# Rows of two batches in one output tile: interleaved on alternate partitions, or one batch in each half

## The chip, the cores and the metric

The kernel runs on one core of a Trainium2 chip. The metric is the device time of one execution in microseconds (us). Eight runs of the kernel before have a median of 428.32 us (427.91 to 428.47).

## What is computed

Sliding-window causal attention over 8 batches, 8 heads, 576 positions and 64 channels per head, followed by a spectral mixing layer. Cut to what matters:

```python
scores = q @ k^T / sqrt(64), kept where 0 <= i - j < 64
x = softmax(scores) @ v                    # as (batch 8, position 576, channel 512)
X = np.fft.rfft(x, axis=1)
Yr = Xr @ w_r[m] - Xi @ w_i[m]             # for the 64 lowest modes m, 512 x 512 each
Yi = Xr @ w_i[m] + Xi @ w_r[m]
y = np.fft.irfft(Y, n=576, axis=1)
u = x + y
out = u + np.maximum(u @ w_ch, 0.0)        # w_ch is 512 x 512
```

All inputs and the output are float32. The output is 8 x 576 x 512, 9.4 MB; the mode weights `w_r` and `w_i` are 64 matrices of 512 x 512 each.

## The kernel before

**Row tiles.** A batch has 576 positions: four whole tiles of 128 and a remainder of 64. The remainders of two neighbouring batches, `b` even and `b + 1`, share one tile, the *pair tile*, numbered `t = NT - 1 = 4` of the even batch. So there are 36 row tiles: 32 whole ones and four pair tiles.

**Stages.** First attention for all batches, then a Fourier transform into `XQ`. Next come the modes: for each mode two weight tiles of 512 KB (in bf16, cast on the way) are fetched by the GpSimd queue through a ring of buffers, and TensorE multiplies them (line 563, and 762 for the last four modes). Beside the modes run smaller jobs: `channel(i)` computes `x @ w_ch` for a row tile into `Z0`; `spectrum(b)` turns a batch's finished modes into the tiles `Yb` and `yw` that the inverse transform multiplies; `spread` rearranges `x_sb` (see below). When the last weights have been used, the *output stage* begins (from line 845), whose order on all engines is written out by hand.

**Output stage.** For row tile `n` of the list `seq`, `lay(n)` puts the tile's `Z0` into a PSUM bank, `rectify(n)` adds `trigI` times `yw` on TensorE (line 870) and takes the positive part on ScalarE (line 875), and `finish(n)` adds `trigI` times `Yb` on TensorE, adds `x_sb` on VectorE (line 893) into the SBUF tile `ot`, and issues the transfer of `ot` to the output on the sync queue (SP). `rectify` runs three tiles ahead of `finish`. In `seq` the pair tiles stand at n = 8, 13, 22 and 27. The pool of `ot` has seven tiles of 4 KB per partition.

**Whole tiles and their transfers.** Two whole row tiles are stored together: partition `p` holds positions `2p` and `2p + 1` of 256, so that each partition sends 4 KB in a row (line 900, 512 KB). The table `trigI` is laid out for that order, and `spread(b, h)` brings `x_sb` into it with four matmuls and two copies for each 256 positions, in the modes from `M0 = 48` to `ME = 60`.

**The pair tile before.** Partition `2s` holds position `512 + s` of the even batch and partition `2s + 1` the same position of the odd one. Four things make it so. `channel` reads the transposed tile with alternating halves (line 592 and 593). The columns of `trigI` from 512 on hold a zero at each even offset and position `512 + s` at offset `2s + 1` (lines 677 to 682); `add` takes 128 columns from 513 for the even batch and from 512 for the odd one (line 869), so that each batch's matmul adds zero to the other's partitions. `spread_pair(b)` rearranges `x_sb` with one matmul against a permutation, `turn`, and one copy (lines 779 to 787). And `finish` sends the tile with one transfer of 128 rows of 2 KB, whose destination alternates between the two batches (line 895).

**The sends.** `send(b)` moves eight rows of 4 KB from the tile `yl` to the last eight partitions of batch `b`'s `Yb` and `yw`, also on the sync queue (line 859). Batch 2 is sent before the first `finish`; `turn_of` (line 909) puts the others after n = 1, 5, 9, 12 and 15. TensorE needs them when it first rectifies a tile of that batch.

Of the kernel before, what the change touches and what calls it, by code (L numbers as in the profile page):

```python
# [9 lines left out]
FP32 = mybir.dt.float32  # L10
FP32R = mybir.dt.float32r
BF16 = mybir.dt.bfloat16
# [8 lines left out]
def view(ap, off, dims):  # L21

    return bass.AP(ap.tensor, ap.offset + off, [list(ap.ap[0])] + [list(d) for d in dims])
# [3 lines left out]
def kernel(  # L27
# [10 lines left out]
    nc = tc.nc  # L38
    B, H, S, D = q.shape
    NM = moe_w_r.shape[0]  # L40
    DM = moe_w_ch.shape[0]
# [3 lines left out]
    NT = 5  # L45
    NC = DM // 128
# [8 lines left out]
    def evac(o, i, on_act):  # L55

        if on_act:
            return nc.scalar.copy(out=o, in_=i)  # L58
        return nc.vector.tensor_copy(out=o, in_=i)  # L59
# [4 lines left out]
    wl = ExitStack()  # L64
# [3 lines left out]
    ident_bf = consts.tile([128, 128], BF16, name="ident_bf")  # L68
# [437 lines left out]
    M0 = L0 * MG  # L506
# [65 lines left out]
    with ExitStack() as p2a:  # L572
# [4 lines left out]
        def channel(i):  # L577
            b, t = tiles[i]
            n = 1 if t == NT - 1 else 2
            psts = []  # L580
            for k in range(n):
                pst = ps_t.tile([128, NC, 128], BF16, name="pxt")
                for c in range(NC):
                    nc.tensor.transpose(out=pst[:, c, :], in_=x_sb[:, b, t + k, 128 * c:128 * c + 128],  # L584
                                        identity=ident_bf)
                psts.append(pst)
            for j in range(n):
                xT = xtp.tile([128, NC, 128], FP32R, name="xT")
                for k in range(n):
                    w = 128 // n  # L590
                    nc.vector.tensor_copy(out=xT[:, :, w * k:w * k + w],  # L591
                                          in_=view(psts[k], j, [[128, NC], [n, w]] if n > 1 else
                                                   [[128, NC], [1, 64], [64, 2]]))
                psz = ps_z.tile([128, DM], FP32, name="psz")
                for c in range(NC):
                    nc.tensor.matmul(out=psz, lhsT=xT[:, c, :], rhs=wch[:, c, :],  # L596
                                     start=(c == 0), stop=(c == NC - 1))
                nc.scalar.copy(out=channel_out(i + j), in_=psz)  # L598
            return n
# [3 lines left out]
        for m in range(L0 * MG):  # L603
# [13 lines left out]
            if m == Z_M - 2:  # L617

                with tc.tile_pool(name="tmpi", bufs=1, reuse_waits="tile") as tmp:
# [23 lines left out]
                    for tab, row in ((trigI, pcol),):  # L643
                        fa, fb = floor(2 * MG, row, "fa"), floor(MG, row, "fb")

                        gcol, mcol = col("gcol"), col("mcol")
                        nc.vector.scalar_tensor_tensor(out=gcol, in0=fa, scalar=-2.0, in1=fb,
                                                       op0=ALU.mult, op1=ALU.add)
                        nc.vector.tensor_tensor(out=mcol, in0=fa, in1=fb, op=ALU.subtract)
                        nc.vector.scalar_tensor_tensor(out=mcol, in0=mcol, scalar=float(MG), in1=row,  # L650
                                                       op0=ALU.mult, op1=ALU.add)
                        for at, dg, dm in ((112 + ML, 1.0, -float(ML)), (112 + MG, -1.0, float(MG)),
                                           (112 + 2 * ML, -1.0, 0.0), (112 + 2 * ML + NLM, 1.0, -float(NLM))):
                            step = col("step")
                            nc.vector.tensor_single_scalar(out=step, in_=row, scalar=at - 0.5, op=ALU.is_ge)
                            nc.vector.scalar_tensor_tensor(out=gcol, in0=step, scalar=dg, in1=gcol,
                                                           op0=ALU.mult, op1=ALU.add)
                            if dm:
                                nc.vector.scalar_tensor_tensor(out=mcol, in0=step, scalar=dm, in1=mcol,
                                                               op0=ALU.mult, op1=ALU.add)  # L660
                        coef, coefs, coefc = col("coef"), col("coefs"), col("coefc")
                        nc.vector.tensor_single_scalar(out=coef, in_=mcol, scalar=0.0, op=ALU.is_equal)
                        nc.vector.tensor_scalar(out=coef, in0=coef, scalar1=-1.0 / S, scalar2=2.0 / S,
                                                op0=ALU.mult, op1=ALU.add)
                        nc.vector.tensor_tensor(out=coefs, in0=gcol, in1=coef, op=ALU.mult)
                        nc.vector.tensor_tensor(out=coefc, in0=coef, in1=coefs, op=ALU.subtract)
                        for i in range(NT):
                            n = SW if i < NT - 1 else 64
                            mt2 = tmp.tile([128, 2, SW], FP32, name="mti")[:, :, 0:n]
                            mt = mt2[:, 0, :]  # L670
                            nc.vector.tensor_scalar(out=mt, in0=pos[:, 0:SW] if n == SW else pos[:, SW:],
                                                    scalar1=float(256 * (i // 2) + i % 2) if n == SW else 0.0,
                                                    scalar2=mcol, op0=ALU.add, op1=ALU.mult)
                            tis = tmp.tile([128, SW], FP32, name="tis")[:, 0:n]
                            gen_trig(tmp, mt2, n, mt, tis, "i")
                            nc.vector.tensor_scalar(out=tis, in0=tis, scalar1=coefs, scalar2=None, op0=ALU.mult)
                            o = SW * i if n == SW else 513
                            nc.vector.scalar_tensor_tensor(out=view(tab, o, [[1 if n == SW else 2, n]]), in0=mt, scalar=coefc, in1=tis,
                                                           op0=ALU.mult, op1=ALU.add)
                    nc.vector.tensor_scalar(out=view(trigI, 512, [[2, 65]]),  # L680
                                            in0=view(trigI, 0, [[1, 65]]), scalar1=0.0,
                                            scalar2=None, op0=ALU.mult)
                    nc.vector.tensor_scalar(out=view(YTl, R - RL, [[R, NC * B], [1, RL]]),
                                            in0=view(trigI, 0, [[RL, NC * B], [1, RL]]), scalar1=0.0,
# [91 lines left out]
        for j in range(2):  # L776
            evac(x_sb[:, b, 2 * h + j, :], ps[j], j)

    def spread_pair(b):

        psj = lo.tile([128, DM], FP32, name="psj", tag="s2")
        nc.tensor.matmul(out=psj, lhsT=turn, rhs=x_sb[:, b, NT - 1, :], start=True, stop=True)
        evac(x_sb[:, b, NT - 1, :], psj, b % 4 == 0)

    spreads = [(b, h) for b in range(B) for h in range(2 + (b % 2 == 0))]
    turn = wl.enter_context(tc.tile_pool(name="turn", bufs=1)).tile([128, 128], BF16, name="turn")
    nc.vector.tensor_copy(out=view(turn, 0, [[2, 64], [1, 2]]), in_=view(ident_bf, 0, [[1, 64], [64, 2]]))

    with tc.manual_schedule(engines={mybir.EngineType.PE}):
        for m in range(M0, ME):  # L790
            while len(spreads) > 5 * B // 2 * (ME - 1 - m) // (ME - M0):
                b0, h = spreads.pop(0)
                spread(b0, h) if h < 2 else spread_pair(b0)
            if (m - M0) % 2 == 0 and (m - M0) // 2 < B // 2:
                b0 = m - M0
                mode(m, lambda: spectrum(b0))
                spectrum(b0 + 1)
            else:
                mode(m)
            if m == M0 + B - 2:  # L800
                wy = late.tile([128, 3, NC, DM], BF16, name="wy", tag="yt")
                free.extend([(wy, j, NM) for j in range(3)])
                refill_w(m, 1)
# [41 lines left out]
    with tc.manual_schedule(engines={mybir.EngineType.PE, mybir.EngineType.Activation, mybir.EngineType.DVE,  # L845
# [20 lines left out]
        def add(n, what, stop):  # L866
            b, t = seq[n]
            for bb, r0, k in parts_of(b, t):
                tr = 128 * t + (t == NT - 1 and r0 == 0)
                nc.tensor.matmul(out=tps[n], lhsT=trigI[:, tr:tr + 128], rhs=pair_tile(what, bb),  # L870
                                 start=False, stop=stop and r0 + k == 128, skip_group_check=True)

# [6 lines left out]
        def finish(n):  # L879
# [12 lines left out]
                return  # L892
            nc.vector.tensor_tensor(out=ot[:, j], in0=ps, in1=x_sb[:, b, t, :], op=ALU.add)  # L893
            if t == NT - 1:
                nc.sync.dma_start(out=out[b:b + 2, 128 * t:, :].rearrange("i s e -> s i e"), in_=ot[:, 0])
            elif n == NQ - 2:
                nc.sync.dma_start(out=out[b, 128 * t:128 * t + 256, :].rearrange("(p j) e -> p j e", j=2)[:, 0],
                                  in_=ot[:, 0])
            elif j:
                nc.sync.dma_start(out=out[b, 128 * t - 128:128 * t + 128, :].rearrange("(p j) e -> p j e", j=2),  # L900
                                  in_=ot)
# [50 lines left out]
```

The softmax here doesn't subtract the row's maximum and nothing guards it: scores larger than these inputs give would overflow.

## Time and profile before

| What | us |
|---|---|
| median of eight runs | 428.32 |
| the profiled execution | 428.37 |
| its span, first to last instruction | 426.6 |
| TensorE busy in the span | 320.7 |
| VectorE busy | 178.1 |
| ScalarE busy | 165.2 |
| line 893, VectorE, 35 adds into `ot`, 0.686 each | 22.2 |
| line 870, TensorE, 80 matmuls, 0.402 each | 23.1 |
| line 875, ScalarE, 36 activations, 0.596 each | 19.2 |
| line 900, transfer of 512 KB, from issue to landing (median) | 4.4 |
| line 895, the pair tile's transfer of 256 KB, issue to landing (median) | 3.8 |

A busy time is a sum over the whole span, in which the stages have different limits; the share of the span says little about what a change in one stage is worth. The profile also holds the records of single transfer packets and of the moments at which a transfer's completion is counted; where a number comes from those, the text says so. The times of transfers "from issue" begin when the queue takes the instruction up, its wait for the data included. PE is TensorE, PEld its weight loads, DVE VectorE, ACT ScalarE, POOL GpSimd and SP the sync engine; a "q" after the name means the engine's instruction queue.

### The profile page before, as it was taken

To read this page: it belongs to the slowest core of one execution; us is meant where nothing else is said; L and a number is where in the kernel's file an instruction comes from. 1 tells how busy PE (TensorE), PEld (TensorE's weight loads), DVE (VectorE), ACT (ScalarE), POOL (GpSimd) and SP (SyncE) were. 2 spreads that over 40 slices of the span, in tenths; PEclk is the share of its full clock that TensorE was granted. 3 is DMA by queue.
4 is the path that set the end of the run, shared out by engine and by line. 5 is a ranking of instruction groups with operands and counts; after the bars stand their busy time and mean duration, and the time that the engine had idled before them with its cause. 6 is when DMAs were issued, how large, how long until landed. Compare 5 with 4: busy or idle time off the path is not lost.

```text
span 426.6 us, 11631 instructions
## 1 busy us (share of the span) xinstructions
PE 320.7 (75%) x5179; PEld 231.0 (54%) x5190; DVE 178.1 (42%) x375; ACT 165.2 (39%) x292; POOL 89.4 (21%) x171
## 2 busy tenths in 40 slices
PE   6999998999989876222497888776458775498993
PEld 5665665666656675112376666654245543266781
DVE  6466766676663100306333332331113322240994
ACT  4575866866773121001031322122103222130992
POOL 7131321231021321211122122121211123200000
PEclk9999999999995855555598896899557866579998
DMA  7999999999999999999999999999999999994598
GB/s 141 212 213 212 213 214 212 213 213 212 215 214 214 213 215 260 214 213 214 213 214 214 213 214 214 213 213 215 212 212 215 214 213 214 215 212 82 202 390 312
DMA packets 28657, 92.16 MB, mean 216 GB/s; under 512 B 2832, under 2 KB 3088, under 8 KB 28608
## 3 DMA queue, kind: packets, MB, share of 16 engines
q0 software_dynamic: 25344, 81.80, 96.2%
q1 hardware_dynamic: 3120, 9.50, 5.8%
q8 instruction: 40, 0.66, 0.6%
q10 hardware_dynamic: 144, 0.13, 0.1%
q14 instruction: 9, 0.07, 0.0%
HBM read 162.53 MB, written 9.44 MB: 403 GB/s over the span
## 4 chain that ended last, share of the span: by engine, by line
DMA 52%; PE 32%; DVE 7%; issue 4%; ACT 2%; POOL 1%; DVEq 0%; POOLq 0%
DMA wt<-in_moe_w_r_dram 26%; DMA wt<-in_moe_w_i_dram 22%; PE pso L316 6%; PE pst L218 6%; DMA wy<-in_moe_w_i_dram 4%; PE pso L870 4%; PE psv L235 3%; DVE x_sb L324 3%; PE pss L272 2%; PE pss L372 2%; PE psx L338 2%; PE pss L291 2%; DVE vT L59 2%; PE psw L711 1%; PE psz L596 1%
## 5 line engine op out<-in xcount | busy, mean ns | idle before, releaser
L563 PE MATMUL psy<-XQ,wt 128*128 128x16 bf16 x1616 | 60.9, 191 | 74.4 <-DMA wt<-in_moe_w_i_dram 37.0
L563 PEld LDWEIGHTS <-wt 128*128 128x128 bf16 x1616 | 52.7, 103 | 88.8 <-DMA wt<-in_moe_w_i_dram 42.3
L591 DVE CAST xT<-pxt 128x256 fp32r<-128x256 bf16 (+1 forms) x68 | 26.3, 435 | 60.1 <-PE pxt L584 40.0
L115 POOL DMA_DIRECT2D wt<-in_moe_w_r_dram x54 | 28.9, 535 | 89.5 <-DMA wt<-in_moe_w_r_dram 43.6
L598 ACT CAST Z<-psz 128x512 fp32r<-128x512 f32 x36 | 21.1, 586 | 65.9 <-PE psz L596 65.9
L115 POOL DMA_DIRECT2D wt<-in_moe_w_i_dram x52 | 28.0, 538 | 86.0 <-DMA wt<-in_moe_w_i_dram 47.3
L596 PE MATMUL psz<-wch,xT 128*128 128x512 f32 x144 | 45.9, 462 | 0.0
L297 ACT ACTIVATE et<-pss 128x512 bf16<-128x512 f32 x72 | 39.2, 601 | 12.8 <-PE pss L291 12.8
L316 PE MATMUL pso<-vt,et 128*64 128x65 bf16 (+1 forms) x576 | 34.0, 209 | 5.2 <-DVE x_sb L324 5.1
L316 PEld LDWEIGHTS <-et 128*64 128x64 bf16 (+1 forms) x576 | 23.7, 113 | 17.2 <-issue 9.8
L596 PEld LDWEIGHTS psz<-wch,xT 128*128 128x128 f32 x144 | 29.5, 220 | 5.8 <-ACT Z L598 0.3
L324 DVE TENSOR_TENSOR x_sb<-pso,rcp 128x640 bf16<-128x640 f32 x32 | 26.3, 822 | 0.9
L870 PE MATMUL pso<-Y,trigI 128*128 128x512 f32 x80 | 23.1, 402 | 0.1
L893 DVE TENSOR_TENSOR ot<-pso,x_sb 128x512 f32<-128x512 f32 x35 | 22.2, 686 | 1.5 <-PE pso L870 1.1
L59 DVE CAST x_sb<-psj 128x512 bf16<-128x512 f32 x18 | 12.3, 689 | 24.7 <-PE psj L773 21.4
L58 ACT CAST YT<-psy 128x256 fp32r<-128x256 f32 x6 | 2.2, 372 | 51.8 <-DVE YT L59 51.8
L272 PE MATMUL pss<-band,ident_bf 64*64 64x512 bf16 x136 | 20.4, 407 | 1.5 <-ACT et L297 1.5
L59 DVE CAST YT<-psy 128x256 fp32r<-128x256 f32 x6 | 2.6, 425 | 43.9 <-PE psy L563 43.9
L59 DVE COPY vT<-pst 128x768 bf16<-128x768 bf16 x16 | 15.3, 958 | 13.0 <-PE pst L218 13.0
L58 ACT CAST x_sb<-psj 128x512 bf16<-128x512 f32 x18 | 10.5, 585 | 24.8 <-PE psj L773 24.4
L875 ACT ACTIVATE pso<-pso 128x512 f32<-128x512 f32 x36 | 19.2, 596 | 0.0
L870 PEld LDWEIGHTS pso<-Y,trigI 128*128 128x128 f32 x80 | 14.5, 188 | 5.5 <-ACT pso L875 1.7
(160 smaller groups left out, 496.3 us busy)
## 6 DMA issues: line engine op xcount, KB each, us to landing
wt<-in_moe_w_r_dram POOLq DMA_DIRECT2D x54, 512.0 KB, 19.1
wt<-in_moe_w_i_dram POOLq DMA_DIRECT2D x52, 512.0 KB, 19.1
out_dram<-ot SPq DMA_DIRECT2D x15, 512.0 KB, 4.4
rk<-in_k_dram POOLq DMA_DIRECT2D x8, 576.0 KB, 10.8
rq<-in_q_dram POOLq DMA_DIRECT2D x8, 576.0 KB, 14.5
rv<-in_v_dram POOLq DMA_DIRECT2D x8, 576.0 KB, 13.1
wy<-in_moe_w_r_dram POOLq DMA_DIRECT2D x3, 512.0 KB, 16.7
wy<-in_moe_w_i_dram POOLq DMA_DIRECT2D x3, 512.0 KB, 19.1
```

What stands on the lines that cost most here:

```text
L59: return nc.vector.tensor_copy(out=o, in_=i)
L115: nc.gpsimd.dma_start(out=wt, in_=src[m].rearrange("(p c) e -> p c e", c=NC))
L218: nc.tensor.transpose(out=ps[64 * hh:64 * hh + 64, c, :], in_=src[:, hh, (c0 + c) * D:(c0 + c + 1) * D], identity=ident_bf)
L272: nc.tensor.matmul(out=pss[(2 * w + hh) % 3][64 * half:64 * half + 64, :], lhsT=ident_bf[pp, pp], rhs=view(band[pp], 128 * half, [[0, WIN ...
L297: nc.scalar.activation(out=et[:, hh, :], in_=pss[(2 * w + hh) % 3], func=ACT_F.Exp, scale=EX_SCALE)
L316: nc.tensor.matmul(out=pso[po, hh, (i // 2) * VW:(i // 2) * VW + D + 1], lhsT=et[pk, hh, col:col + 64], rhs=vt[pk, 1 - f % 2, 2 * hh + g / ...
L324: nc.vector.tensor_tensor(out=view(x_sb, b * NT * DM + g * D, [[4 * D, 2], [DM, NT], [1, D]]), in0=view(pso, 0, [[512, 2], [VW, NT], [1, D]]),
L563: nc.tensor.matmul(out=psy[:, m % MG, e, :], lhsT=w[:, c, 128 * e:128 * e + 128], rhs=XQ[:, c, :, 1 - im:3 - im, m], start=(m % MG == im + ...
L591: nc.vector.tensor_copy(out=xT[:, :, w * k:w * k + w], in_=view(psts[k], j, [[128, NC], [n, w]] if n > 1 else [[128, NC], [1, 64], [64, 2]]))
L596: nc.tensor.matmul(out=psz, lhsT=xT[:, c, :], rhs=wch[:, c, :], start=(c == 0), stop=(c == NC - 1))
L870: nc.tensor.matmul(out=tps[n], lhsT=trigI[:, tr:tr + 128], rhs=pair_tile(what, bb), start=False, stop=stop and r0 + k == 128, skip_group_c ...
L893: nc.vector.tensor_tensor(out=ot[:, j], in0=ps, in1=x_sb[:, b, t, :], op=ALU.add)
```

## The change

The pair tile holds the even batch's 64 positions on partitions 0 to 63 and the odd batch's on 64 to 127. The alternating read in `channel`, `spread_pair`, `turn` and its copy are gone. `trigI` holds 64 zero columns, the 64 columns of positions 512 to 575 and 64 zero columns; `add` starts at 576 for the even batch and at 512 for the odd one. `finish` sends a pair tile with two transfers of 64 rows of 2 KB, one for each batch, both on the sync queue. The 16 spreads that remain are dealt out over the same 12 modes. `send` and `turn_of` are the same in both versions, although the change is also described as sending the last rows of the batches more spread out.

```diff
                 for k in range(n):
                     w = 128 // n
-                    nc.vector.tensor_copy(out=xT[:, :, w * k:w * k + w],
-                                          in_=view(psts[k], j, [[128, NC], [n, w]] if n > 1 else
-                                                   [[128, NC], [1, 64], [64, 2]]))
+                    nc.vector.tensor_copy(out=xT[:, :, w * k:w * k + w], in_=view(psts[k], j, [[128, NC], [n, w]]))
...
-                            o = SW * i if n == SW else 513
-                            nc.vector.scalar_tensor_tensor(out=view(tab, o, [[1 if n == SW else 2, n]]), in0=mt, scalar=coefc, in1=tis,
+                            o = SW * i if n == SW else 576
+                            nc.vector.scalar_tensor_tensor(out=tab[:, o:o + n], in0=mt, scalar=coefc, in1=tis,
                                                            op0=ALU.mult, op1=ALU.add)
-                    nc.vector.tensor_scalar(out=view(trigI, 512, [[2, 65]]),
-                                            in0=view(trigI, 0, [[1, 65]]), scalar1=0.0,
+                    nc.vector.tensor_scalar(out=view(trigI, 512, [[128, 2], [1, 64]]),
+                                            in0=view(trigI, 0, [[64, 2], [1, 64]]), scalar1=0.0,
...
-    def spread_pair(b):
-
-        psj = lo.tile([128, DM], FP32, name="psj", tag="s2")
-        nc.tensor.matmul(out=psj, lhsT=turn, rhs=x_sb[:, b, NT - 1, :], start=True, stop=True)
-        evac(x_sb[:, b, NT - 1, :], psj, b % 4 == 0)
-
-    spreads = [(b, h) for b in range(B) for h in range(2 + (b % 2 == 0))]
-    turn = wl.enter_context(tc.tile_pool(name="turn", bufs=1)).tile([128, 128], BF16, name="turn")
-    nc.vector.tensor_copy(out=view(turn, 0, [[2, 64], [1, 2]]), in_=view(ident_bf, 0, [[1, 64], [64, 2]]))
+    spreads = [(b, h) for b in range(B) for h in range(2)]
...
-            while len(spreads) > 5 * B // 2 * (ME - 1 - m) // (ME - M0):
-                b0, h = spreads.pop(0)
-                spread(b0, h) if h < 2 else spread_pair(b0)
+            while len(spreads) > 2 * B * (ME - 1 - m) // (ME - M0):
+                spread(*spreads.pop(0))
...
-                tr = 128 * t + (t == NT - 1 and r0 == 0)
+                tr = 128 * t + (64 - r0 if t == NT - 1 else 0)
...
-                nc.sync.dma_start(out=out[b:b + 2, 128 * t:, :].rearrange("i s e -> s i e"), in_=ot[:, 0])
+                for i, queue in enumerate((nc.sync, nc.sync)):
+                    queue.dma_start(out=out[b + i, 128 * t:, :], in_=ot[64 * i:64 * i + 64, 0])
```

## The prediction

> **What bounds the kernel now.** I read the page's slices first, then the chain of waits, then tables of short stretches, then the sync queue's timeline. One profiled execution took 428.37 us, 1.77 us more than its span of 426.6; the median of the eight runs is 428.32, so a change of the span is carried over as it is.
>
> ```profile
> span 426.6 us, 11631 instructions
> ...
> DMA  7999999999999999999999999999999999994598
> GB/s 141 212 213 212 213 214 212 213 213 212 215 214 214 213 215 260 214 213 214 213 214 214 213 214 214 213 213 215 212 212 215 214 213 214 215 212 82 202 390 312
> ```
>
> The transfer engines are full from the second slice to the 36th, at 212 to 215 GB/s: that is the stream of weights. Two slices are thin, and the last two run at 390 and 312 GB/s: that is the output. So the kernel has a load stage that ends near 391 us and an output stage of 35 us, and I ask in each what ends last. In the chain of waits the seam reads:
>
> ```profile
> 372.30 19.13 DMA wy<-in_moe_w_i_dram
> 391.44 0.05 issue
> 391.48 0.66 PE psl L762 x16
> 392.17 0.23 DVE YT L847
> ```
>
> The last weight tile lay 19.13 us in the queue, and TensorE had to wait for it (its idle time before L762 ends with that landing). Nothing that TensorE, VectorE or ScalarE do before 391 us sets this moment, as long as the queue stays that deep. The output stage, in stretches (busy us of each engine, granted clock, DMA share, GB/s):
>
> ```profile
> core 0: us, PE busy (x) PEld busy (x) DVE busy (x) ACT busy (x) POOL busy (x), PEclk, DMA share, GB/s
> 399.00:402.00 3.00, 3.00 (x14) 2.28 (x13) 2.62 (x5) 3.00 (x7) 0.00 (x0) 1.00 0.84 277
> 402.00:405.00 3.00, 3.00 (x14) 2.40 (x14) 2.79 (x5) 3.00 (x7) 0.00 (x0) 1.00 1.01 393
> 405.00:408.00 3.00, 3.00 (x14) 2.43 (x14) 2.90 (x5) 3.00 (x7) 0.00 (x0) 1.00 1.00 397
> 408.00:411.00 3.00, 3.00 (x15) 2.41 (x14) 2.80 (x6) 3.00 (x7) 0.00 (x0) 1.00 0.95 370
> 411.00:414.00 3.00, 3.00 (x15) 2.42 (x14) 2.70 (x5) 3.00 (x7) 0.00 (x0) 1.00 1.01 401
> 414.00:417.00 3.00, 3.00 (x15) 2.42 (x14) 2.89 (x6) 2.99 (x7) 0.00 (x0) 1.00 1.02 401
> 417.00:420.00 3.00, 2.40 (x9) 1.19 (x7) 3.00 (x6) 1.84 (x4) 0.00 (x0) 1.00 1.01 396
> 420.00:423.00 3.00, 0.00 (x0) 0.00 (x0) 0.69 (x3) 0.00 (x0) 0.00 (x0) 1.00 1.02 402
> ```
>
> All three compute engines are full until 417, and so are the transfers. Compute ends at 420.7; the transfers run on at 402 GB/s to about 424.5. In the records of single packets, summed by tenths of a us, the 16 engines stand idle 0.17 us in all between 404.9 and 408.9, 0.18 us between 408.9 and 411.5, and practically nothing after that. **So from 411.5 us the output transfers set the end**: whatever makes a transfer longer there is added one for one, and before that the first 0.35 us are absorbed. Of the 3.8 us from the last VectorE result (420.7) to the last large packets (424.5), about 1.15 is the way from a result to its first packets (398.26 to 399.4 for the first output transfer) and 0.32 the last 128 KB at 400 GB/s. The rest, 2.3 us, is backlog: compute could be that much later at its end and cost nothing.
>
> **Part one: work taken away before 391 us.** Gone are four weight loads L782 (98 to 146 ns) with a matmul each (the matmuls are missing from the trace; the nearest rows, L773's 512-column ones, take 376 to 636 ns), two VectorE copies of 692 ns, two ScalarE copies of 585 ns, and the 228 ns copy that makes `turn`. Sum: TensorE 4 x (0.12 + 0.41) = 2.1 us, VectorE 1.6, ScalarE 1.2. The four pair-tile casts of L591 (up to 692 ns, 128x512) now read in a straight line, the zero fill L680 (190 ns) goes from 65 to 128 columns, and the trig columns are written with step 1: tenths of a us either way. The other spreads are dealt out anew over the 12 modes from 48. All of it lies under the weight stream, which runs at 211 to 217 GB/s in each 5 us from 280 to 385; I take 0. If that cover were gone, TensorE's 2.1 us would be the gain; that is the lower bound. The dummy matmuls that precede the seam are untouched, and the granted clock is 1.00 from 380 on, so I change nothing in TensorE's rate.
>
> **Part two: operands of the pair tiles in the output stage.** Same eight matmuls from other columns of `trigI`, same VectorE add: 0.
>
> **Part three: eight transfers in place of four.** The sync queue is where they are issued:
>
> ```profile
> 406.96 1.12 SPq L895 DMA_DIRECT2D out_dram<-ot  x1
> 408.17 0.55 SPq L900 DMA_DIRECT2D out_dram<-ot  x1
> 408.82 0.65 SPq L859 DMA_DIRECT2D Y<-yl  x1
> ```
>
> Such an issue includes its wait: L895 here starts at 406.96, but the VectorE result it needs comes at 408.08. Without a wait an issue takes 0.33 to 0.55 us (L900 at 405.42, 408.17, 419.46). The second half therefore adds about 0.5 us to the queue, four times. Behind it stand the next output issue and, after n = 13, `send(7)`; behind `send(7)` the queue waits for VectorE again (409.94), so the delay dies out there. At n = 22 and 27 the next issue waits for VectorE anyway (414.31, 417.59): 0. The added completion writes, 16 of 4 bytes for each transfer at 8.4 ns, come to 4 x 8.4 = 0.03 us per engine.
>
> The real question is the transfer itself. Each pair tile is 128 packets of 2 KB in both versions; now a median packet takes 84 ns, so a pair tile is 8 packets per engine, 0.67 us. But a half reads only 64 adjacent partitions. The trace has no such transfer. Lower bound: nothing lost, as in L895 over 128 partitions, 400 GB/s. The other row is `send`, which moves 4 KB from and to eight adjacent partitions: with no output beside it, its eight packets (398.79 to 399.44) took 255 to 572 ns, where an output packet of that size takes 159, and 32 KB in 0.65 us is 50 GB/s. Few adjacent partitions can thus hold transfers back. Read per partition, that row (6.3 GB/s each) would let 64 partitions give 400 GB/s, no loss; scaled from the 128-partition row (3.1 GB/s each), 64 give 200, and a pair tile takes 1.34 us in place of 0.67. Upper bound: +0.67 each. 64 lies nearer to 128 than to 8, so I lean to the upper end, but not wholly: the packets of one pair tile start over 1.0 to 1.7 us (404.84 to 406.54 for the first), so engines are not in step, and some will read one half while others read the other. I take 0.5.
>
> [...]
>
> Sum: 4 x 0.5 = 2.0, less the 0.35 us of idle before 411.5 that the first two pair tiles fill, plus 0.03: **+1.7 us, 428.37 + 1.7 = 430.0**. Bounds: 4 x 0.67 = 2.7 with nothing absorbed gives 431.1; no loss gives 428.4.
>
> **Where the delay goes on the way.** The sends share the queue with the output. By the completion counts `send(7)` lands at 412.18, and TensorE's first load that waits for it is at 412.47, 0.29 us of slack; `send(6)` has 1.8. With two pair tiles ahead, `send(7)` is later by about 2 x 0.5 - 0.17 = 0.8 us, so TensorE should stand some 0.5 us there, with every later tile behind it. VectorE then ends near 421.2. The backlog of 2.3 us covers that; it isn't added. The short name of the change speaks of sends more spread out; `turn_of` is the same in both versions, so no gain is counted from it.
>
> **Rivals.**
> - *The halves cost nothing* (the other side: not slower). The engines run apart and the two halves use different partitions, so neighbours in the queue fill in. For it: packets of one tile spread over more than a us. Against it: the send's 572 ns. It decides as soon as the average loss is under 0.3 us a pair tile. Then 428.4 (0.03 us of completion writes), up to 429.0 if `send(7)` is late by the 0.5 us of issue. Chance 0.27.
> - *The spreads were on the path after all.* If the weight queue ran dry because its buffers were freed late, 2.1 us of TensorE come back: 426.3. It decides where L762 no longer waits for a landing. Against it: 19 us from issue to landing. Chance 0.04.
> - *Stall and transfer add up.* If the late `send(7)` empties the queue near 413, the 0.5 us of TensorE come on top of the upper bound: 431.1 + 0.5 = 431.6. For it: the backlog near 412 is still small. Chance 0.07.
> - The forecast, a loss between 0.25 and 0.67 us a pair tile, has the rest, 0.62; its own range is 429.2 to 431.1.
>
> **How the numbers follow.** 0.2% is 0.86 us, about what the runs can tell from no change. Slower: 0.62 + 0.07 + 0.03 of the first rival = 0.72; same: the other 0.24; faster 0.04. The range 428.3 to 431.0 takes in the first rival and leaves out the two extremes and a little of the forecast's top.
>
> **What would show it.** Right: 2 KB packets of the pair tiles near 150 ns; the last VectorE result within 1 us of 420.7, but the last packets near 426; TensorE idle before L870 at n = 27. Wrong: packets still at 84 ns, or the seam at 391.48 moved, or the transfers idle after 411.5.

## The result and the profile after

The changed kernel takes 430.18 us (median of ten runs, 429.37 to 430.77), the kernel before 428.34 in the same comparison: a ratio of 1.0040, 95% interval 1.0032 to 1.0048. It is slower by 1.7 us (1.4 to 2.1). The forecast was 430.0. The profiled execution took 430.25 us with a span of 428.2. These are its slices on the page, DMA share in tenths and GB/s:

```profile
span 428.2 us, 11629 instructions
...
DMA  7999999999999999999999999999999999992698
GB/s 142 212 213 213 213 214 212 214 212 213 214 214 210 214 214 260 214 213 214 213 214 213 214 214 213 215 214 213 213 214 213 214 214 214 213 213 54 248 352 302
```

The weight stream is what it was. The last two slices carry 352 and 302 GB/s in place of 390 and 312. The chain of waits, start and length in us, says the same of the seam, and shows a piece that the kernel before did not have:

```profile
372.05 19.14 DMA wy<-in_moe_w_i_dram
391.19 0.05 issue
391.24 0.66 PE psl L760 x16
...
409.69 0.05 issue
409.74 0.03 SPq L848
409.76 0.03 issue
409.79 3.54 DMA Y<-yl
413.33 0.04 issue
413.38 0.50 PE pso L859
```

TensorE starts on the last weights at 391.24 (before: 391.48), so nothing was lost or won in the load stage. At 413.33 `send(7)` lands, late, and TensorE goes on at 413.38. The stretches of the output stage, in the same columns as before:

```profile
core 0: us, PE busy (x) PEld busy (x) DVE busy (x) ACT busy (x) POOL busy (x), PEclk, DMA share, GB/s
402.00:405.00 3.00, 3.00 (x14) 2.37 (x13) 2.79 (x5) 3.00 (x8) 0.00 (x0) 1.00 1.01 388
405.00:408.00 3.00, 3.00 (x14) 2.44 (x13) 2.90 (x6) 3.00 (x8) 0.00 (x0) 1.00 0.89 333
408.00:411.00 3.00, 3.00 (x14) 2.40 (x14) 2.80 (x5) 3.00 (x8) 0.00 (x0) 1.00 0.98 330
411.00:414.00 3.00, 2.25 (x10) 1.50 (x10) 2.05 (x4) 2.08 (x6) 0.00 (x0) 1.00 0.98 367
414.00:417.00 3.00, 3.00 (x15) 2.45 (x14) 2.54 (x4) 3.00 (x7) 0.00 (x0) 1.00 0.92 330
417.00:420.00 3.00, 3.00 (x12) 1.81 (x10) 3.00 (x6) 2.59 (x6) 0.00 (x0) 1.00 1.01 384
```

Two different losses can be told apart here. From 408 to 411 the engines are busy (0.98) and move only 330 GB/s: packets are slower. From 405 to 408 and from 414 to 417 the share itself falls, to 0.89 and 0.92: engines stand idle. The sync queue's timeline (start, length of the merged issues) shows what happened ahead of the first dip:

```profile
402.69 1.88 SPq L885 DMA_DIRECT2D out_dram<-ot  x2
404.67 0.68 SPq L848 DMA_DIRECT2D Y<-yl  x1
405.46 0.85 SPq L890 DMA_DIRECT2D out_dram<-ot  x2
```

The two halves hold the queue for 1.88 us, where the one transfer held it for 0.65. Taken singly in the trace, the second half is issued from 403.39 to 404.57, although its data has been there since 402.44, when VectorE's add for n = 8 ended. The semaphore that this issue waits for, that of an older transfer, had its last count at 399.63. At the third pair tile the queue reads as follows, the kernel before first:

```profile
412.23 0.98 SPq L895 DMA_DIRECT2D out_dram<-ot  x1
413.43 1.90 SPq L900 DMA_DIRECT2D out_dram<-ot  x2
415.71 0.82 SPq L895 DMA_DIRECT2D out_dram<-ot  x1
```

```profile
411.13 1.79 SPq L890 DMA_DIRECT2D out_dram<-ot  x2
413.01 2.66 SPq L885 DMA_DIRECT2D out_dram<-ot  x2
415.76 1.02 SPq L890 DMA_DIRECT2D out_dram<-ot  x2
```

To say who waits for whom here, one has to know whether the length of an issue holds its wait for the data. It doesn't. In the kernel before, eleven output issues find the queue idle, and each of them starts 0.03 us after the end of the VectorE add that completes its tile (n = 24: 413.40 and 413.43); in neither kernel does one start before that. So the wait lies ahead of the row, contrary to what the part on the time before and the prediction say, and the length, 0.33 to 1.19 us in the kernel before, is the issue itself. The distance from the last add of a tile to its issue then tells whether the queue keeps up. For the whole tile that follows each pair tile it is, in us:

| profiled execution | behind n = 8 | behind 13 | behind 22 | behind 27 |
|---|---|---|---|---|
| before | 0.78 | 0.69 | 0.03 | 0.03 |
| after | 1.82 | 1.94 | 2.62 | 1.56 |

In the kernel before the queue has caught up with VectorE by 411.44; in the changed kernel it never does: from the first pair tile on, no issue finds the queue idle.

The records of single packets give the sizes. "Stage" is the time from the first matmul on the last weight tile to the end of the large packets (the last sixteen left out); "packets" is the duration of all packets in it, divided by 16; "idle" is the engines' idle time from 10 to 30.5 us after that matmul, summed by tenths of a us.

| profiled execution | stage | packets | idle | 2 KB packets of the pair tiles: time on an engine, four tiles | VectorE's last result after the seam |
|---|---|---|---|---|---|
| before | 33.02 | 25.16 | 0.34 | 0.68, 0.70, 0.68, 0.68 | 29.21 |
| after | 35.15 | 26.45 | 0.95 | 0.81, 1.00, 0.92, 1.00 | 30.21 |

So the stage is 2.1 us longer: 1.29 us of slower packets and 0.61 of idle time make up 1.9 of it. The seam came 0.24 us earlier and the close after the last packets was 0.29 shorter (428.2 - 426.39 against 426.6 - 424.50), which leaves the 1.6 us between the spans. Of the packets of the pair tiles, 195 of 512 took more than 120 ns, with a second cluster near 150; before, none of the four tiles had more than two.

### The profile page after: what moved, and what is told of

Read it like the earlier page. It is cut to its first block, busy times and chain, and to the rows that moved or that the text cites. A ratio compares the mean times of both kernels' runs of the same rounds, so it can differ in the third digit from the quotient of the medians.

```text
span 428.2 us, 11629 instructions
## 1 busy us (share of the span) xinstructions
PE 321.6 (75%) x5179; PEld 230.0 (54%) x5186; DVE 176.3 (41%) x372; ACT 164.2 (38%) x290; POOL 89.3 (21%) x171
## 4 chain that ended last, share of the span: by engine, by line
DMA 55%; PE 28%; DVE 8%; issue 4%; ACT 2%; POOL 1%; DVEq 0%; POOLq 0%; SPq 0%
DMA wt<-in_moe_w_i_dram 48%; PE pso L316 7%; PE pst L218 6%; DMA wy<-in_moe_w_i_dram 4%; PE psv L235 3%; DVE x_sb L324 3%; PE pss L372 3%; PE pso L859 2%; PE pss L272 2%; DMA wt<-in_moe_w_r_dram 2%; DVE ot L882 2%; PE psx L338 2%; PE pss L291 2%; DVE vT L59 2%; ACT vt L58 1%
## 5 line engine op out<-in xcount | busy, mean ns | idle before, releaser
L594 PE MATMUL psz<-wch,xT 128*128 128x512 f32 x144 | 44.9, 454 | 0.0
L59 DVE CAST x_sb<-psj 128x512 bf16<-128x512 f32 x16 | 11.0, 688 | 27.4 <-PE psj L771 27.3
L58 ACT CAST x_sb<-psj 128x512 bf16<-128x512 f32 x16 | 9.4, 586 | 27.0 <-PE psj L771 27.0
## 6 DMA issues: line engine op xcount, KB each, us to landing
rq<-in_q_dram POOLq DMA_DIRECT2D x8, 576.0 KB, 12.7
```

## The experiments

My theory after the result: two causes, slow packets from 64 adjacent partitions, and a sync queue that is held by one more transfer for each pair tile. The rivals: each of the two alone. All ratios are to the kernel before, timed on the same chip, with 95% intervals.

**Two transfers, but from every second partition.** In the kernel before:

```diff
-                nc.sync.dma_start(out=out[b:b + 2, 128 * t:, :].rearrange("i s e -> s i e"), in_=ot[:, 0])
+                for i in range(2):
+                    nc.sync.dma_start(out=out[b + i, 128 * t:, :], in_=ot[i:128:2, 0])
```

> The kernel before, with each pair tile sent in two transfers of 64 rows, one for each batch, taken from every second partition. Same number of transfers, rows and destinations as in the changed kernel; only the place of the rows differs. If 64 adjacent partitions are what lengthens the transfers: median packet of 2 KB near 84 ns with next to none above 120, time within 0.5 us of the kernel before (428.3 to 428.8). If the number of transfers and issues on the sync queue costs it: 429.5 to 430.5, as the changed kernel. [...]

Measured: 429.41 us, 1.0022 (1.0012 to 1.0031). The packets are at 84 ns again (7 above 120), and yet about 1 us is lost, more than adjacency alone allowed: idle is 1.03, as in the changed kernel, the stage 33.97. The tiles behind the pair tiles are issued 1.84, 1.87, 2.22 and 1.47 us after their adds. Adjacency is not the whole of it.

**Two transfers of all 128 partitions, half of the channels each.**

```diff
-                nc.sync.dma_start(out=out[b:b + 2, 128 * t:, :].rearrange("i s e -> s i e"), in_=ot[:, 0])
+                for c0 in (0, DM // 2):
+                    cc = slice(c0, c0 + DM // 2)
+                    nc.sync.dma_start(out=out[b:b + 2, 128 * t:, cc].rearrange("i s e -> s i e"), in_=ot[:, 0, cc])
```

> The kernel before, with each pair tile sent in two transfers of 128 rows of 1 KB (the two halves of the channels). Number of transfers as in the changed kernel, all partitions in each. 1 KB packets take 46 ns in the kernel before, so 4 x (16 x 46 - 8 x 84) = 0.26 us per engine more. Theory of adjacent partitions: 428.3 + 0.3, up to 428.8. Theory of issues on the sync queue: 429.5 or more, with issues of about 1.2 us for the second transfers.

Measured: 429.53 us, 1.0028 (1.0013 to 1.0043); idle 0.94, stage 34.17. The second issues take 1.17, 0.60, 1.33 and 1.07 us. A second transfer costs about a us in four pair tiles, here with rows over all partitions too; the smaller packets, 0.27 us more on each engine, are a part of it.

**A second transfer that moves almost nothing.** The same cut at 480 of the 512 channels:

```diff
-                for c0 in (0, DM // 2):
-                    cc = slice(c0, c0 + DM // 2)
+                for cc in (slice(0, 480), slice(480, DM)):
```

> The kernel before, with each pair tile sent in two transfers of all 128 partitions, the first of 1,920 B a row, the second of 128 B a row. If a transfer takes a place in the sync queue whatever its size, the small one costs what a half costs: 429.2 to 429.8, with second issues of 0.6 to 1.4 us. If only the short lookahead in bytes counts, about half of that: 428.7 to 429.0. If neither: 428.4.

Measured: 429.70 us, 1.0023 (1.0008 to 1.0038); idle 0.94, stage 34.16. The timeline of the sync queue:

```profile
403.11 1.81 SPq L896 DMA_DIRECT2D out_dram<-ot  x2
405.03 0.72 SPq L859 DMA_DIRECT2D Y<-yl  x1
```

128 B a row hold the queue as long (1.81 us for the pair, second issues of 1.11, 0.60, 1.31 and 1.25) as half a tile does. It is the transfer that counts, not its bytes.

**The second alternate transfer from the GpSimd queue.** To the first experiment:

```diff
-                for i in range(2):
-                    nc.sync.dma_start(out=out[b + i, 128 * t:, :], in_=ot[i:128:2, 0])
+                for i, queue in enumerate((nc.sync, nc.gpsimd)):
+                    queue.dma_start(out=out[b + i, 128 * t:, :], in_=ot[i:128:2, 0])
```

> The run with two transfers from every second partition, the second of them issued by the GpSimd queue, which is idle in the output stage and so delays nothing else. As many transfers as there, as many sync issues as in the kernel before. If the extra idle time comes from the places and issues of the sync queue: idle of the transfers before 422 us falls from 1.2 to 0.45 to 0.7 us, the large packets end at 424.5 to 425.0 (425.6 with both on the sync queue), the time is 428.5 to 429.0 with some 0.4 us for a later close of the GpSimd queue in it. If the number of transfers costs it whoever issues them: 425.6 and 429.4 or more.

Measured: 428.74 us against 428.53 for the kernel before beside it, 0.9999 (0.9988 to 1.0010): the loss is gone. The sync queue's timeline at the same place:

```profile
403.66 0.56 SPq L896 DMA_DIRECT2D out_dram<-ot  x1
404.33 0.80 SPq L859 DMA_DIRECT2D Y<-yl  x1
405.23 1.12 SPq L901 DMA_DIRECT2D out_dram<-ot  x2
```

One issue of 0.56 us, and idle back at 0.34, the stage at 33.13 (the absolute end, 425.2, is later than expected because this execution's seam came at 392.07). The tiles behind the pair tiles are issued 0.76, 0.88, 0.04 and 0.03 us after their adds, as in the kernel before. The GpSimd queue sends its half as 32 packets of 4 KB (two rows each) in place of 64 of 2 KB, but that is not the gain: its four halves take 1.31 us of each engine's time, the four on the sync queue 1.38. Eight transfers in place of four cost nothing that the interval can tell (0.4 us) when the sync queue does not have to issue them all. With the three runs above this settles the first cause: **the sync queue's hold, about 1 us**.

**Halves, with the second from the GpSimd queue.** The same, in the changed kernel:

```diff
-                for i, queue in enumerate((nc.sync, nc.sync)):
+                for i, queue in enumerate((nc.sync, nc.gpsimd)):
```

> The changed kernel, with the second half of each pair tile issued by the GpSimd queue in place of the sync queue. The partitions are the same 64. If the slow packets carry the loss, the time stays within 0.6 us of the changed kernel's 430.2. If the 1.2 us for which the second issue holds the sync queue carries it, the idle time of the transfers falls by 0.5 us or more and the time goes to 428.5 to 429.3.

Measured: 429.95 us, 1.0039 (1.0024 to 1.0054): no gain. Idle falls to 0.52, but the packets take 26.74 us, 0.29 more than in the changed kernel, and the stage stays at 35.14. Beside the run before, which differs from it in where the rows lie (and in the rearranging, which a run below shows to be hidden), this is adjacency without a second issue on the sync queue: 1.0039 against 0.9999, some 1.7 us. On the sync queue the same step, from every second partition to halves, costs 0.8 us (1.0022 to 1.0040). So the two causes don't simply add: 1.0 and 1.7 alone, 1.7 together. Between the two runs with the GpSimd queue the packets take 1.50 us more of each engine's time, of which its own 4 KB packets make 0.83 (267 ns in the mean against 163), the 2 KB packets on the sync queue 0.35 and all others 0.3; the same step on the sync queue makes 0.99. So part of the difference lies in the GpSimd queue's larger packets; why a half costs more beside a half in another queue was not tested.

**Whole tiles cut too, in halves and in rows.** The suspected cost eight times over. In the changed kernel each 512 KB transfer is cut by partitions, in the kernel before into two of all partitions:

```diff
-                nc.sync.dma_start(out=out[b, 128 * t - 128:128 * t + 128, :].rearrange("(p j) e -> p j e", j=2),
-                                  in_=ot)
+                to = out[b, 128 * t - 128:128 * t + 128, :].rearrange("(p j) e -> p j e", j=2)
+                for pp in (slice(0, 64), slice(64, 128)):
+                    nc.sync.dma_start(out=to[pp], in_=ot[pp])
```

```diff
+                to = out[b, 128 * t - 128:128 * t + 128, :].rearrange("(p j) e -> p j e", j=2)
+                for i in range(2):
+                    nc.sync.dma_start(out=to[:, i], in_=ot[:, i])
```

> The changed kernel, with each of the 15 whole-tile transfers (512 KB) also cut into two of 64 adjacent partitions with 4 KB rows. Both theories at once, eight times the rows of the pair tiles: adjacency costs 0.2 to 0.5 us for each 256 KB, the extra issue 0.25 us each. Expected 428.4 + 1.8 + 30 x (0.2 to 0.5) + up to 15 x 0.25: 438 to 449. If the pair tiles' loss came from their place in the order alone: under 434.

> The kernel before, with each of the 15 whole-tile transfers cut into two of all 128 partitions with 2 KB rows: the same number of transfers as the run with halves, without adjacency. If the sync queue holds about five transfers at a time whatever their size, 15 more cost about 0.25 us each: 431 to 433 (of which 0.5 us is 2 KB packets being slower than 4 KB ones). If the count costs nothing: 428.4 to 429.

Measured: halves 442.23 us, 1.0336 (1.0313 to 1.0358); rows 430.67 us, 1.0061 (1.0046 to 1.0076). One stretch of each, halves first, in the columns of the stretches above:

```profile
408.00:412.00 4.00, 3.90 (x18) 2.84 (x17) 3.11 (x5) 3.49 (x7) 0.00 (x0) 1.00 0.86 233
```

```profile
408.00:412.00 4.00, 4.00 (x19) 3.21 (x18) 3.70 (x7) 4.00 (x9) 0.00 (x0) 1.00 0.95 357
```

With the same number of transfers the halves move 233 GB/s and the rows 357. Cutting the 15 whole tiles costs 12.7 us in halves (over the changed kernel, 1.0336 - 1.0040) and 2.6 in rows. The 4 KB packets average 233 ns in the halves, 171 in the changed kernel. Over 1,968 packets and 16 engines that is 7.6 us, 0.25 for each of the 30 x 256 KB: the price that the packets of the pair tiles show too (1.0 us for four). Idle time of the engines, 4 us more, comes on top, in a stage in which TensorE waits up to 3.8 us for a late send and the granted clock is 0.51 from 420 to 424; so the 10 us between the two runs aren't all the packets' own. That the place of the rows lengthens the packets is settled, and with it the second cause, **adjacent partitions**.

**Sends earlier.** In the changed kernel:

```diff
-        turn_of = {1: 3, 5: 4, 9: 5, 12: 6, 15: 7}
+        turn_of = {1: 3, 5: 4, 7: 5, 9: 6, 11: 7}
```

> The changed kernel with batches 5, 6 and 7 sent after n = 7, 9 and 11 in place of 9, 12 and 15, so that send(7) stands ahead of the second pair tile. If TensorE's wait of 0.8 to 1.1 us for send(7) is covered by the backlog, as predicted: the wait is gone, VectorE ends 0.5 us or more earlier, the time stays within 0.4 us of 430.2. If the wait sits on the path: 429.2 to 429.6.

Measured: 429.79 us, 1.0041 (1.0028 to 1.0054), as the changed kernel. The waits of TensorE's weight loads in the output stage (us in total, times, longest), the changed kernel first:

```profile
PEld pso L859 <- ACT pso L864: 1.7, 6, 0.4
...
PEld pso L859 <- DMA Y<-yl: 1.1, 1, 1.1
```

```profile
PEld pso L859 <- ACT pso L864: 1.7, 6, 0.4
PEld pso L859 <- ACT Y L851: 0.4, 1, 0.4
PEld pso L859 <- ACT pso L752: 0.4, 2, 0.2
```

The wait for `Y<-yl` is gone and VectorE's last result is 29.23 us after the seam again, 1.0 us earlier, but the time stays within what the interval can tell (the median is 0.4 us lower, the ratio the same). The wait that the chain names was covered by the backlog of the transfers; the interval leaves room for 0.5 us of it at most.

**No spread of the pair tiles.** The kernel before without `spread_pair` and `turn`:

```diff
-    spreads = [(b, h) for b in range(B) for h in range(2 + (b % 2 == 0))]
+    spreads = [(b, h) for b in range(B) for h in range(2)]
...
-            while len(spreads) > 5 * B // 2 * (ME - 1 - m) // (ME - M0):
-                b0, h = spreads.pop(0)
-                spread(b0, h) if h < 2 else spread_pair(b0)
+            while len(spreads) > 2 * B * (ME - 1 - m) // (ME - M0):
+                spread(*spreads.pop(0))
```

> The kernel before without the four matmuls and copies that bring the pair tiles' rows of x into the alternating order (the output's last 64 rows of each batch are left wrong for it); this is the work that the change takes away in the load stage. Prediction: it lies under the weight stream, so no change, 428.3 within 0.3, with the first matmul after the last weight tile at 391.2 to 391.7. Rival: it was on the path, up to 2.1 us faster, 426.2.

Measured: 428.32 us, 0.9998 (0.9989 to 1.0007), seam at 391.33. The rearranging that the change removes was hidden.

**The sends from the GpSimd queue.** In `send` of the changed kernel, `nc.sync` becomes `nc.gpsimd`.

> The changed kernel with the six sends issued by the GpSimd queue, so that they take no place in the sync queue. If the places of the sync queue cost about 1 us: idle time of the transfers falls by 0.3 us or more, issues of the second halves get shorter, 429.3 to 429.8. If they don't: 430.2 within 0.3.

Measured: 430.19 us, 1.0041 (1.0029 to 1.0053). Idle falls to 0.62 and the stage to 34.15, 1.0 us less than in the changed kernel, but the time does not follow: the span is again 428.2, with 2.4 us from the last large packets to its end in place of 1.8, and the seam of this execution came 0.3 us later. TensorE now waits 0.9 to 1.3 us for a send. Fewer transfers on the sync queue shorten the stage, as the theory says, but the expected 429.3 to 429.8 was missed; why the close is longer I did not follow further.

**The second transfer from ScalarE's queue.** Two runs meant to free the sync queue: `(nc.sync, nc.scalar)` in place of `(nc.sync, nc.sync)`, once with every second partition, once with halves.

> The run with two transfers from every second partition, but the second of them issued by ScalarE's queue, so that the sync queue holds as many transfers as in the kernel before. If the places of the sync queue cause the 0.6 us of extra idle time: idle of the transfers before 422 us falls from 1.2 towards 0.45 us, no sync issue of a pair tile holds the queue for 1.2 us, and the time goes from 429.4 to 428.4 to 428.9 (ScalarE gives four issues of some 0.4 us, in a stage whose end has 2.3 us of backlog). If the number of transfers as such costs it, whoever issues them: 429.4 as before.

> The changed kernel with the second half of each pair tile issued by ScalarE's queue. What is left then is adjacency alone: slow 2 KB packets as in the changed kernel (mean 100 to 125 ns), idle time before 422 us near 0.5. Theory of two causes that add: 429.1 to 429.6. Theory that the slow packets carry all of it: 430.2. Theory that the queue carries all of it: 428.5.

Measured: 431.76 us, 1.0079 (1.0065 to 1.0093), and 432.22 us, 1.0087 (1.0073 to 1.0100). Both expectations missed, for a reason that has nothing to do with the question. The waits of the first:

```profile
PEld pso L870 <- ACT pso L875: 4.1, 13, 0.8
PEld pso L870 <- ACT pso L754: 3.6, 6, 1.3
ACT pso L754 <- DVE ot L893: 2.0, 2, 1.1
```

In ScalarE's queue the transfer has to wait for VectorE's `ot`, and the copies behind it (L754) then wait for it too, 2.0 us in all; TensorE waits for them, and idle grows to 3.2 us. The runs say nothing of the sync queue.

## Why the prediction was right

**The bound and the stage: right.** The loss lies wholly in the output stage, whose transfers set the end; compute ends 1.0 us later after the seam and is covered, as the run with earlier sends shows.

**Part one at nothing: shown** by the run without the spread, 0.9998.

**The transfer itself, +0.5 us for a pair tile: the mechanism right, the size too large.** The four tiles' own packets took 0.13, 0.30, 0.24 and 0.32 us longer, 1.0 in all where 2.0 were forecast, and other packets 0.3. "2 KB packets near 150 ns" held for 155 of 512 (120 to 170 ns; 40 more took longer); 278 stayed under 90, so the median of 84, one of the prediction's own signs of being wrong, did not move. The 0.5 was my estimate, between no loss and the 0.67 scaled from a row of 128 partitions; no run shows it. The packets show 0.25 us a tile, in the pair tiles and where all tiles are cut in halves, and the place of the rows alone made 1.7 us between the two runs with the GpSimd queue.

**The step that failed: "so the delay dies out there", and "At n = 22 and 27 ... 0".** Its root is a misread row. "Such an issue includes its wait" is wrong: L895 at 406.96 carries n = 13, whose add had ended at 406.18; 408.08 is the end of a later add, for n = 16. So its 1.12 us are the issue itself, and the 0.33 to 0.55 us that I took for an issue were the short ones. The kernel before has long ones in plain sight, with the data there since 420.36:

```profile
421.10 1.19 SPq L891 DMA_DIRECT2D out_dram<-ot  x1
```

By the same misreading I saw waits for VectorE up to 409.94, 414.31 and 417.59 in which a delay could vanish. At 409.94 there was none: that issue carries n = 17, whose add had ended at 408.73. Behind the pair tiles n = 22 and 27 the queue was idle for 0.2 and 0.5 us, from the end of one issue to the next. The second issues took 1.18, 0.59, 1.46 and 1.21 us, more than that, and the queue stayed behind, by up to 2.62 us. Priced alone this is 1.0 us, and it was forecast at nothing.

What holds an issue so long stays open. The ends of the issues never show more than five of the queue's transfers under way in these two kernels, whatever their size (six in the run with rows), and two of the four second issues end within 0.05 us of an older transfer's landing (404.57 both for the first). But the third ends at 415.67 with three others under way, 1.1 us after the last landing, so a fixed number of places doesn't explain it. That a small transfer costs what a large one does, and that the cost goes when the GpSimd queue issues it, is shown.

**The 0.35 us of idle time to be filled: wrong.** Idle went up by 0.61, to 0.95; in the three runs with a second transfer on the sync queue from all partitions or from every second one it was 0.94 to 1.03, so the slow packets of the halves filled nothing that shows. The engines' share fell to 0.92 between 414 and 417, where it was 1.02: "the transfers idle after 411.5" was another of the prediction's signs of being wrong. So the total came out right by luck in part, with one term twice too large and another missing.

**`send(7)`: right in kind, larger in size.** TensorE's wait was put at 0.5 us and is 0.8 to 1.1. It was said to be covered, and it is.

**The rivals.** That the halves cost nothing is refuted, yet its "up to 429.0" for delays of the queue is near what the two-transfer runs measured (429.4 to 429.7). The spreads were not on the path, and stall and transfer did not add up.

## What to carry to other kernels

Where a stage is bound by its output transfers, count transfers as well as bytes: with three or four others under way, a further one on the same queue held that queue for 0.6 to 1.5 us here, 1.3 even with 128 B a row. Whether a queue keeps up is read from the distance between the end of the work that makes the data and the start of the issue; where the queue is idle, that distance also shows whether a row's length holds its wait. Here a transfer did best spread over all partitions: 0.68 us on an engine for a pair tile in one transfer, 0.81 to 1.00 in halves. Rows of two destinations can be put on alternate partitions so that one transfer serves both, if the rearranging is done where engines have slack (the kernel before without it: 0.9998). The GpSimd queue, which had nothing else to do in this stage, could take the extra transfer (0.9999 with every second partition); ScalarE's, whose engine had its own work behind it, could not (1.0079).

## What was not expected of the hardware

The cost of a transfer that moves 16 KB in 128 B rows: 1.0 us over four pair tiles, as much as one of 128 KB. And the packets of a half fall into two groups, near 84 and near 150 ns, with only 38% over 120 ns; why the others are not slowed is not shown. The price was 0.25 us of packet time for 256 KB in the pair tiles, and no higher where all tiles were cut in halves.
